# Alternate split units, the second vv from SBUF, and A loads ahead of C loads

## The chip, the cores and the metric

The kernel runs on one core of one Trainium2 chip. The metric is the device time of one execution in microseconds: before the change the median of three runs is 690.73 us (689.88 to 691.08). The page and the trace come from one further, profiled execution.

Engines are named as in the profile: PE is TensorE's matmul and PEld its weight load, DVE is VectorE, ACT is ScalarE, POOL is GpSimd, SP is SyncE, which here only issues DMAs. "PEq", "SPq" and so on are their sequencers.

## The reference

`x` is 8 batches of 3008 rows of 256. Each batch goes through a two-dimensional Fourier transform, of which the real part is kept, and then through a gated feed-forward block with 1536 hidden columns:

```python
def _attn_ref(x):
    X = np.fft.fft(x, axis=1)
    X = np.fft.fft(X, axis=2)
    return X.real

def _moe_ref(x, w_gate, w_val, w_out):
    g = x @ w_gate
    silu = g * (1.0 / (1.0 + np.exp(-g)))
    val = x @ w_val
    return silu * val @ w_out
```

Output: 24064 rows of 256, float32.

## The kernel before

**The mathematics that the kernel uses.** Rows k and M - k of the transform share their cosine and sine products. The kernel therefore computes half of the rows of each batch (H = 1504) as a pair of columns, one in Pt (the part that has the same sign in both rows) and one in Qt (the part whose sign turns), and the feed-forward block makes both output rows from the pair. The transform along the 256 columns is folded into the weights: Wp and Wq are the gate and value weights times cosines and sines, and Wm is Wq times -2 (0 in row 0).

**Folds and transforms.** The rows of x are added and subtracted before they are multiplied. A batch has two sets of rows, A and C, loaded into XA and XC. `fold_steps` gives seven steps for one half of a set: SDf (sum and difference, L165), EOf (L168, L169, L172), Af (L175), CE (L178, L179) and BB (L182 to L184). All run on POOL. `transform` (L559 on) multiplies CE and BB with the tables on PE, ACT copies one half (od, L599), and DVE puts sums and differences into Pt and Qt (L604). `spread` fixes in which unit each fold step is issued, `slot` in which unit each transform.

**Units.** The 12032 pairs are cut into 24 tiles: six of 480 or 512 columns for the first two batches, then 512 each, and 320 in the last (tile 23), which also carries 8 columns for row 0 of each batch. A tile has 12 units, one for each 128 of the hidden columns. The main loop walks over all units. For each it issues some loads on SP (`run_loads`), the unit's first part (`part_a`), four matmuls of the output product of the tile before (`OWork.run`), the second part of the unit before (`part_b`), four more output matmuls, and the fold steps and transforms due. Every engine works through its instructions in this order.

**An unsplit unit** has six matmuls of a tile's width: g and v of the plus row (Wp on Pt, Wq on Qt), then, in `part_b`, Wm on Qt added on top of both, which makes g and v of the minus row. ACT takes Silu of g each time (L764, L782) and DVE multiplies with v straight from PSUM into hp and hm (L765, L783).

**A split unit** has five. e = Wp on Pt and o = Wm on Qt go to two PSUM banks of their own. DVE makes es = e + w0 * bc in SBUF (L752), then vv = es - o/2 for the plus row, called vp in the code (L754), and vv = es + o/2 for the minus row, called vm (L756). Since v is now in SBUF, POOL can make the products hp and hm (L757, L779), with Silu from ACT (L749, L778). bc is row 0 of Qt spread over all partitions: one matmul with `sel` (L880) and an ACT copy (L883) for each tile.

`split(u)` says which units are split: in tiles 3 to 22, units 0, 2, 3, 5, 7 and 9 of a tile, and in tiles 21 and 22 nine of the twelve (`SPLIT_END`). There are 126 in all.

**Buffers.** vv has four buffers (two for each split unit), sgv four, es two, bc two; the PSUM pools of g and v have three banks each, that of the output product two. The evicted output ev has four buffers (L703, L706), which SP stores to DRAM (L709).

**Loads.** `loads` is a list. `load_next` appends the loads of a set as soon as its buffer has been read: 20 for A of one batch (L129, L131), 78 for C of two batches (L140, L143, L145). In each unit `run_loads` issues the first three of the list if A stands at its head, else six. The first fold step of a set issues what is left of its loads and all that stands ahead of them in the list. SP also issues the stores, in the order of the program.

Of the kernel before, what the change touches and what calls it, by code (L numbers as in the profile page):

```python
# [16 lines left out]
Alu = mybir.AluOpType  # L17
# [14 lines left out]
def kernel(  # L32
# [8 lines left out]
    nc = tc.nc  # L41
    B, M, D = x.shape
# [14 lines left out]
    nT = len(wide)  # L57
# [9 lines left out]
    def width(t):  # L67
        return wide[t]

    def tile_of(c):  # L70
        return max(t for t in range(nT) if t0[t] <= c)
# [46 lines left out]
    def up_block(b, j, n):  # L118
        return rows_at(b, 2 * j - 1, [[2 * D, n], [R * D, 4], [1, 2 * D]])

    def down_set(b, a, j, L, n):

        return rows_at(b, R * (a + 1) - 2 * j, [[2 * L * D, n], [-2 * D, L], [1, 2 * D]])
# [3 lines left out]
    def load_a(b, q):  # L127
        X3 = XA.rearrange("p a q d -> p a (q d)")
        return ([lambda h=h: q.dma_start(out=X3[LA * h:LA * (h + 1), 0:4, :],  # L129
                                         in_=up_block(b, JA - LA * h, LA)) for h in range(NA)] +  # L130
                [lambda a=a: q.dma_start(out=X3[:, 4 + a, :], in_=down_set(b, a, JA, LA, NA)) for a in range(4)])  # L131

    def load_c(b, q):
        bb = b % 2
        steps = []
        for qq in range(2):
            p0 = 64 * qq
            for h in range(NC_):
                up = rows_at(b, 2 * (JC - LC * h) - 1 + qq, [[2 * D, LC], [R * D, 4], [1, D]])
                steps.append(lambda p=p0 + LC * h, up=up: q.dma_start(out=XC[p:p + LC, 0:4, bb, :], in_=up))  # L140
            for a in range(4):
                down = rows_at(b, R * (a + 1) - 2 * JC + 1 - qq, [[2 * LC * D, NC_], [-2 * D, LC], [1, D]])
                steps.append(lambda p=p0, a=a, down=down: q.dma_start(out=XC[p:p + NCR, 4 + a, bb, :], in_=down))  # L143
        pm = 64 + NCR
        steps.append(lambda: q.dma_start(out=XC[pm:pm + 1, 0:4, bb], in_=rows_at(b, 0, [[R * D, 1], [R * D, 4], [1, D]])))  # L145
        return steps
# [381 lines left out]
    def pq_tiles(t):  # L528
        if t not in ptile:
            w = width(t) + B if t == nT - 1 else T  # L530
            ptile[t] = (pqp if t < nT - 1 else const).tile([P, w], BF16, name="Pt")
            qtile[t] = (pqp if t < nT - 1 else const).tile([P, w], BF16, name="Qt")
        return ptile[t], qtile[t]
# [181 lines left out]
    state = {}  # L715
    owork = None

    SPLIT = (0, 2, 3, 5, 7, 9)
    SPLIT_END = (0, 1, 2, 4, 5, 7, 8, 10, 11)
    t_end = tile_of((B - 1) * H) + 1  # L720

    bc = {}

    def split(u):

        return 3 <= u[0] < nT - 1 and u[1] in (SPLIT if u[0] < t_end else SPLIT_END)

    def part_a(u):
        t, f = u
        w = width(t) + (B if t == nT - 1 else 0)  # L730
        fs = slice(f * P, (f + 1) * P)
        if f == 0:
            hts[t] = (hp.tile([P, nF, T + B], BF16, name="hp"), hp.tile([P, nF, T], BF16, name="hm"))
        Pt, Qt = pq_tiles(t)

        def mm(ps, Wt, gv, src, start, stop):
            nc.tensor.matmul(ps[:, :w], Wt[:, gv, fs], src[:, :w], start=start, stop=stop,  # L737
                             skip_group_check=True)

        g = psG.tile([P, T], F32, name="g")  # L740
        mm(g, Wp, 0, Pt, True, False)
        mm(g, Wq, 0, Qt, False, True)
        if split(u):
            e = psV.tile([P, T], F32, name="v")
            mm(e, Wp, 1, Pt, True, True)
            o = psV.tile([P, T], F32, name="v")
            mm(o, Wm, 1, Qt, True, True)
            sg = sgv.tile([P, T], F32, name="sgv")
            nc.scalar.activation(sg[:, :w], g[:, :w], AF.Silu)  # L749
            stt = nc.vector.scalar_tensor_tensor  # L750
            es = esp.tile([P, T], F32, name="es")
            stt(es[:, :w], bc[t][:, :w], w0[:, f:f + 1], e[:, :w], op0=Alu.mult, op1=Alu.add)  # L752
            vp = vvp.tile([P, T], F32, name="vv")
            stt(vp[:, :w], o[:, :w], -0.5, es[:, :w], op0=Alu.mult, op1=Alu.add)  # L754
            vm = vvp.tile([P, T], F32, name="vv")
            stt(vm[:, w - 1::-1], o[:, :w], 0.5, es[:, :w], op0=Alu.mult, op1=Alu.add)  # L756
            nc.gpsimd.tensor_tensor(hts[t][0][:, f, :w], sg[:, :w], vp[:, :w], op=Alu.mult)  # L757
            state[u] = (g, vm)
            return
        v = psV.tile([P, T], F32, name="v")  # L760
        mm(v, Wp, 1, Pt, True, False)
        mm(v, Wq, 1, Qt, False, True)
        sg = sgp.tile([P, T], F32, name="sg")
        nc.scalar.activation(sg[:, :w], g[:, :w], AF.Silu)  # L764
        nc.vector.tensor_tensor(hts[t][0][:, f, :w], sg[:, :w], v[:, :w], op=Alu.mult)  # L765
        state[u] = (g, v)

    def part_b(u):
        t, f = u
        w = width(t)  # L770
        Pt, Qt = pq_tiles(t)
        g, v = state.pop(u)
        for gv, ps in ((0, g), (1, v))[:1 if split(u) else 2]:
            nc.tensor.matmul(ps[:, :w], Wm[:, gv, f * P:(f + 1) * P], Qt[:, :w], start=False, stop=True,  # L774
                             skip_group_check=True)
        if split(u):
            sg = sgv.tile([P, T], F32, name="sgv")
            nc.scalar.activation(sg[:, w - 1::-1], g[:, :w], AF.Silu)  # L778
            nc.gpsimd.tensor_tensor(hts[t][1][:, f, :w], sg[:, :w], v[:, :w], op=Alu.mult)  # L779
            return  # L780
        sg = sgp.tile([P, T], F32, name="sg")
        nc.scalar.activation(sg[:, :w], g[:, :w], AF.Silu)  # L782
        nc.vector.tensor_tensor(hts[t][1][:, f, w - 1::-1], sg[:, :w], v[:, :w], op=Alu.mult)  # L783
# [13 lines left out]
    for b in range(2, B, 2):  # L797
        u = slot[(b, 0)] - 1
# [9 lines left out]
    def run_loads(n):  # L808
        for _, fn in loads[:n]:
            fn()  # L810
        del loads[:n]

    def fold_step(what, i, unit):
        kind, b = what
        q, j = divmod(i, 7)
        if i == 0:
            run_loads(max((k + 1 for k, (w_, _) in enumerate(loads) if w_ == what), default=0))
        if j == 0:
            if kind == "A":
                queue[what] = fold_steps(nc.gpsimd, XA, *coef_a(b), q, slice(0, P))  # L820
            else:
                bb = 1 if b == 1 else q
                queue[what] = fold_steps(nc.gpsimd, XC, *coef_c(b), bb, slice(0, P), q_down=bb)
        queue[what].pop(0)()
        if q == LASTQ[kind, b == 1] and j == 1:
            act_at.setdefault(max(unit + 2, 11), []).append(what)

    def load_next(what):
        kind, b = what
        if kind == "A":  # L830
            if b + 1 < B:
                loads.extend((("A", b + 1), fn) for fn in load_a(b + 1, nc.sync))
        else:
            b = b // 2 * 2 + 2
            if b < B:
                loads.extend((("C", b), fn) for fn in load_c(b, nc.sync) + load_c(b + 1, nc.sync))
# [5 lines left out]
    for jb in jobs[1:]:  # L842
        u = slot[jb]
# [27 lines left out]
    loads = []  # L871
# [3 lines left out]
    for i, u in enumerate(units):  # L875
        t, f = u
        if f == 0 and split((t, SPLIT[0])):
            ps = psG.tile([P, T], F32, name="g")
            w = width(t)
            nc.tensor.matmul(ps[:, :w], sel, pq_tiles(t)[1][:, :w], start=True, stop=True)  # L880
            bc.pop(t - 2, None)
            bc[t] = bcp.tile([P, T], F32, name="bc")
            nc.scalar.copy(bc[t][:, :w], ps[:, :w])  # L883
        for fn in before.pop(i, ()):
            fn()
        if i == 10:
            loads[0:0] = ((("A", 1), fn) for fn in load_a(1, nc.sync))
        run_loads(3 if loads and loads[0][0][0] == "A" else 6)
        part_a(u)
        if owork:  # L890
            owork.run(4)
        if prev is not None:
            part_b(prev)
            if prev[1] == nF - 1:
                owork = OWork(prev[0], hts[prev[0]])
                owork.run(4)
        if owork and not (prev is not None and prev[1] == nF - 1):
            owork.run(4)
        for what, j in fold_at.get(i, ()):
            fold_step(what, j, i)  # L900
        for what in act_at.pop(i, ()):
            load_next(what)
        if i in job_at:
            transform(*job_at[i])
        prev = u
# [35 lines left out]
```

## Time and profile before

| what | value |
|---|---|
| median of three runs | 690.73 us |
| profiled execution, its own time | 688.43 us |
| its span on the core | 686.7 us |
| mean granted TensorE clock | 0.995 |
| instructions in the span | 13388 |
| HBM read / written | 29.39 MB / 24.65 MB |
| mean DMA rate over the span | 77 GB/s |

The time is what the runs are compared by; the span is from the first to the last instruction of the profiled execution, and every duration and window of the trace lies within it.

In a group's row stand the line, the engine, the operation, output and inputs, their shapes and the count; behind the bar the busy time in us and the mean ns of one, and behind the next bar the idle time just before them and what ended it. A line number is one of the kernel as printed above. In a timeline's row stand the start and the duration in us, and in brackets how long the engine idled before it and what released it. A row of the waits has who waited for whom, then the total in us, how many times, and the longest.

### The profile page before, as it was taken

Reading aid. Unit: us, or ns where it says so; the run is one execution under the profiler, and the core shown is the slowest. Engines: PE = TensorE matmul, PEld = TensorE weight load, DVE = VectorE, ACT = ScalarE, POOL = GpSimd, SP = SyncE. Lnnn points to the kernel's source line nnn. Section 1 sums busy time; section 2 is a strip of 40 time slices with the busy share of each in tenths; the row PEclk is TensorE's granted clock in tenths of the full one; section 3 lists DMA queues with packets and bytes.
Section 4 is the critical chain, followed back from the end, with each engine's and each line's share of the span. In section 5 each row is a group of like instructions: output and inputs, shape, how many; then the busy total and the mean of one; then the engine's idle time right before and its main releaser. Section 6 shows DMA issues by size and latency. Waiting matters only on the chain.

```text
span 686.7 us, 13388 instructions
## 1 busy us (share of the span) xinstructions
PE 662.1 (96%) x4374; PEld 414.7 (60%) x4374; DVE 513.5 (75%) x919; ACT 432.4 (63%) x764; POOL 570.3 (83%) x558
## 2 busy tenths in 40 slices
PE   7989999999799999999999999999999999999997
PEld 5446665665455666565665666656666666656676
DVE  8886668786567877777777787777777787788862
ACT  7676655665456666565666666666666666666663
POOL 9991977999499999999998998998999655668920
PEclk9999999999989999999999999999999999999999
DMA  9555225323512412235125111117111011111112
GB/s 229 105 87 109 74 59 156 110 67 107 165 31 66 121 47 68 72 95 160 36 62 145 38 44 35 48 40 155 36 48 48 32 41 38 46 32 47 47 47 70
DMA packets 49767, 52.56 MB, mean 77 GB/s; under 512 B 7130, under 2 KB 41026, under 8 KB 49698
## 3 DMA queue, kind: packets, MB, share of 16 engines
q1 hardware_dynamic: 46514, 49.35, 26.4%
q0 software_dynamic: 3184, 2.36, 2.4%
q8 instruction: 34, 0.56, 0.4%
q14 instruction: 35, 0.29, 0.1%
HBM read 29.39 MB, written 24.65 MB: 79 GB/s over the span
## 4 chain that ended last, share of the span: by engine, by line
PE 80%; DVE 8%; POOL 4%; issue 4%; ACT 1%; DMA 1%; SPq 0%; DVEq 0%; ACTq 0%; POOLq 0%
PE o L697 31%; PE v L737 16%; PE g L737 15%; PE g L774 8%; PE v L774 4%; PE v L572 3%; DVE vv L756 2%; DVE Pt L604 1%; PE g L572 1%; POOL hm L779 1%; DVE es L752 1%; DMA out_dram<-ev 1%; DVE vv L754 1%; POOL SDf L165 1%; PE g L880 1%
## 5 line engine op out<-in xcount | busy, mean ns | idle before, releaser
L757 POOL TENSOR_TENSOR hp<-sgv,vv 128x512 bf16<-128x512 f32 (+1 forms) x126 | 160.3, 1274 | 39.9 <-DVE vv L754 26.8
L697 PE MATMUL o<-Wo,hm 128*128 128x256 bf16 (+2 forms) x1140 | 170.5, 274 | 0.0
L697 PE MATMUL o<-Wo,hp 128*128 128x256 bf16 (+2 forms) x1140 | 169.6, 273 | 0.0
L779 POOL TENSOR_TENSOR hm<-sgv,vv 128x512 bf16<-128x512 f32 (+1 forms) x126 | 159.8, 1273 | 9.9 <-ACT sgv L778 8.2
L697 PEld LDWEIGHTS <-hp 128*128 128x128 bf16 (+2 forms) x1140 | 112.0, 98 | 68.2 <-issue 7.8
L697 PEld LDWEIGHTS <-hm 128*128 128x128 bf16 (+2 forms) x1140 | 112.4, 99 | 65.8 <-issue 6.4
L752 DVE SCALAR_TENSOR_TENSOR es<-bc,w,v 128x512 f32<-128x512 f32 (+1 forms) x126 | 93.7, 744 | 52.4 <-PE v L737 52.3
L765 DVE TENSOR_TENSOR hp<-sg,v 128x512 bf16<-128x512 f32 (+2 forms) x162 | 107.8, 665 | 33.0 <-ACT sg L764 32.1
L783 DVE TENSOR_TENSOR hm<-sg,v 128x512 bf16<-128x512 f32 (+2 forms) x162 | 107.4, 663 | 24.2 <-ACT sg L782 15.3
L782 ACT ACTIVATE sg<-g 128x512 f32<-128x512 f32 (+2 forms) x162 | 94.7, 585 | 46.8 <-PE g L774 46.0
L764 ACT ACTIVATE sg<-g 128x512 f32<-128x512 f32 (+2 forms) x162 | 94.5, 583 | 38.2 <-PE g L737 35.6
L737 PE MATMUL v<-Pt,Wp 128*128 128x512 bf16 (+2 forms) x288 | 108.4, 376 | 6.3 <-DVE vv L756 6.2
L737 PE MATMUL g<-Pt,Wp 128*128 128x512 bf16 (+2 forms) x288 | 108.5, 377 | 1.5 <-ACT sgv L778 1.1
L778 ACT ACTIVATE sgv<-g 128x512 f32<-128x512 f32 (+1 forms) x126 | 75.4, 598 | 53.7 <-PE g L774 39.8
L737 PE MATMUL g<-Qt,Wq 128*128 128x512 bf16 (+2 forms) x288 | 108.2, 376 | 0.5 <-DVE Qt L604 0.5
L774 PE MATMUL g<-Qt,Wm 128*128 128x512 bf16 (+2 forms) x288 | 108.1, 375 | 0.0
L754 DVE SCALAR_TENSOR_TENSOR vv<-v,es 128x512 f32<-128x512 f32 (+1 forms) x126 | 87.0, 690 | 18.6 <-POOL hp L757 1.0
L756 DVE SCALAR_TENSOR_TENSOR vv<-v,es 128x512 f32<-128x512 f32 (+1 forms) x126 | 85.7, 680 | 12.9 <-POOL hm L779 12.8
L749 ACT ACTIVATE sgv<-g 128x512 f32<-128x512 f32 (+1 forms) x126 | 75.1, 596 | 30.6 <-PE g L737 23.0
L165 POOL TENSOR_TENSOR SDf<-XA 128x1024 f32<-128x1024 f32 x28 | 66.0, 2363 | 24.8 <-DMA XC<-in_x_dram 14.7
L737 PEld LDWEIGHTS <-Wp 128*128 128x128 bf16 x576 | 56.4, 98 | 45.3 <-issue 7.7
L703 ACT COPY ev<-o 128x512 f32<-128x512 f32 x90 | 52.7, 586 | 34.3 <-PE o L697 29.1
(170 smaller groups left out, 731.0 us busy)
## 6 DMA issues: line engine op xcount, KB each, us to landing
out_dram<-ev SPq DMA_DIRECT2D x96, 128.0 KB
XA<-in_x_dram SPq DMA_DIRECT2D x32, 256.0 KB
XA<-in_x_dram SPq DMA_DIRECT2D x112, 64.0 KB
XC<-in_x_dram SPq DMA_DIRECT2D x210, 16.0 KB
XC<-in_x_dram SPq DMA_DIRECT2D x56, 60.0 KB
out_dram<-ev SPq DMA_DIRECT2D x12, 120.0 KB
out_dram<-ev SPq DMA_DIRECT2D x10, 112.0 KB
XA<-in_x_dram SPq DMA_DIRECT2D x1, 1024.0 KB
```

The lines of the kernel that those rows point to most:

```text
L697: nc.tensor.matmul(ps[:n, j, :], hts[minus][:, f, c:c + n], Wo[:, f, :], start=(f == 0), stop=(f == nF - 1))
L737: nc.tensor.matmul(ps[:, :w], Wt[:, gv, fs], src[:, :w], start=start, stop=stop, skip_group_check=True)
L752: stt(es[:, :w], bc[t][:, :w], w0[:, f:f + 1], e[:, :w], op0=Alu.mult, op1=Alu.add)
L754: stt(vp[:, :w], o[:, :w], -0.5, es[:, :w], op0=Alu.mult, op1=Alu.add)
L756: stt(vm[:, w - 1::-1], o[:, :w], 0.5, es[:, :w], op0=Alu.mult, op1=Alu.add)
L757: nc.gpsimd.tensor_tensor(hts[t][0][:, f, :w], sg[:, :w], vp[:, :w], op=Alu.mult)
L764: nc.scalar.activation(sg[:, :w], g[:, :w], AF.Silu)
L765: nc.vector.tensor_tensor(hts[t][0][:, f, :w], sg[:, :w], v[:, :w], op=Alu.mult)
L774: nc.tensor.matmul(ps[:, :w], Wm[:, gv, f * P:(f + 1) * P], Qt[:, :w], start=False, stop=True, skip_group_check=True)
L779: nc.gpsimd.tensor_tensor(hts[t][1][:, f, :w], sg[:, :w], v[:, :w], op=Alu.mult)
L782: nc.scalar.activation(sg[:, :w], g[:, :w], AF.Silu)
L783: nc.vector.tensor_tensor(hts[t][1][:, f, w - 1::-1], sg[:, :w], v[:, :w], op=Alu.mult)
```

## The change

Four edits are made together.

- `SPLIT` becomes the even units. A new list, `SPLIT_MID`, has eight units and is used in tiles 19 and 20 (`t_folds` is 19). `SPLIT_END`, for tiles 21 and 22, keeps nine units but others. The last tile, which had no split unit, gets the first seven of `SPLIT_MID`; its bc therefore covers the 8 extra columns too.
- The second vv is computed as 2 * es - vp from the two SBUF tiles in place of es + o/2. In the last tile it has the 320 columns of the minus row, while es and vp have 328.
- There are now 96 split units in tiles 3 to 18, 16 in tiles 19 and 20, 18 in tiles 21 and 22, and 7 in tile 23: 137.
- `load_next` puts the loads of A in front of the first C load that is still in the list.

```diff
-    SPLIT = (0, 2, 3, 5, 7, 9)
-    SPLIT_END = (0, 1, 2, 4, 5, 7, 8, 10, 11)
+    SPLIT = (0, 2, 4, 6, 8, 10)
+    SPLIT_END = (0, 1, 3, 4, 6, 7, 9, 10, 11)
+    SPLIT_MID = (0, 1, 3, 4, 6, 7, 9, 10)
     t_end = tile_of((B - 1) * H) + 1
+    t_folds = t_end - 2
...
-        return 3 <= u[0] < nT - 1 and u[1] in (SPLIT if u[0] < t_end else SPLIT_END)
+        t, f = u
+        if t == nT - 1:
+            return f in SPLIT_MID[:-1]
+        return t >= 3 and f in (SPLIT if t < t_folds else SPLIT_MID if t < t_end else SPLIT_END)

     def part_a(u):
         t, f = u
-        w = width(t) + (B if t == nT - 1 else 0)
+        n = width(t)
+        w = n + (B if t == nT - 1 else 0)
...
             vm = vvp.tile([P, T], F32, name="vv")
-            stt(vm[:, w - 1::-1], o[:, :w], 0.5, es[:, :w], op0=Alu.mult, op1=Alu.add)
+            stt(vm[:, n - 1::-1], es[:, :n], 2.0, vp[:, :n], op0=Alu.mult, op1=Alu.subtract)
...
             if b + 1 < B:
-                loads.extend((("A", b + 1), fn) for fn in load_a(b + 1, nc.sync))
+                at = next((k for k, (w_, _) in enumerate(loads) if w_[0] == "C"), len(loads))
+                loads[at:at] = [(("A", b + 1), fn) for fn in load_a(b + 1, nc.sync)]
...
         if f == 0 and split((t, SPLIT[0])):
             ps = psG.tile([P, T], F32, name="g")
-            w = width(t)
+            w = width(t) + (B if t == nT - 1 else 0)
```

In the printed code after the change the lines from L719 on stand 6 or 7 lower: es is L758, vp L760, vm L762, hp on POOL L763, hm on POOL L785.

## The prediction

> **What bounds the kernel now.** I read the page's busy times first, then the chain of waits, then busy time by stage, then the timelines around the places where TensorE stops.
>
> ```profile
> PE 662.1 (96%) x4374; PEld 414.7 (60%) x4374; DVE 513.5 (75%) x919; ACT 432.4 (63%) x764; POOL 570.3 (83%) x558
> ...
> PE 80%; DVE 8%; POOL 4%; issue 4%; ACT 1%; DMA 1%; SPq 0%; DVEq 0%; ACTq 0%; POOLq 0%
> ```
>
> TensorE is the bound: 96% busy, and 80% of the chain. The 83% of POOL is an average over stages that differ, so I cut the span where the first split unit begins (104.4), where the last fold has ended (546), and where POOL has run out of work (654). The columns are the stretch, its length, and busy time and instructions of PE, PEld, DVE, ACT and POOL.
>
> ```profile
> 104.40:546.00 441.60, 428.99 (x2812) 266.05 (x2811) 334.46 (x583) 276.33 (x486) 413.95 (x378) 0.99 0.29 79
> 546.00:654.00 108.00, 106.86 (x703) 66.73 (x702) 87.63 (x148) 70.18 (x122) 72.62 (x58) 1.00 0.13 40
> 654.00:687.00 33.00, 28.88 (x244) 23.81 (x242) 12.70 (x26) 15.48 (x35) 3.72 (x3) 1.00 0.21 61
> ...
> POOL SDf L165 <- DMA out_dram<-ev: 10.0, 1, 10.0
> POOL SDf L165 <- DMA XA<-in_x_dram: 7.9, 1, 7.9
> POOL hp L757 <- DVE vv L754: 7.9, 14, 1.0
> ```
>
> In the fold stage POOL is busy 413.95 of 441.6 us: 27.65 us of slack in all. One wait of 10.0 us is a hole; 2.4 us of the 7.9 us wait (it ends at 106.83, below) lie in the stage. POOL is the second bound here, 3% behind the first. In the last tiles there are no folds and it has 35 us to spare; DVE has 20.
>
> The hole costs TensorE this:
>
> ```profile
> 190.27 0.59 PE L737 MATMUL v<-Pt,Wp 128*128 128x512 bf16 x1 [6.23 <-DVE vv L756]
> ...
> 190.00:200.00 10.00, 9.73 (x46) 5.21 (x46) 6.12 (x11) 4.96 (x10) 10.00 (x10) 0.71 0.08 26
> 200.00:210.00 10.00, 9.86 (x67) 5.61 (x64) 7.49 (x14) 5.45 (x10) 9.92 (x11) 1.00 0.10 28
> ```
>
> 6.23 us of waiting, then ten microseconds at a granted clock of 0.71 in which 46 matmuls ran where the next ten hold 67: another 10 x 21/67 = 3.1 us. Together 9.3 us.
>
> **Part 1: more split units.** A split unit leaves out one 512-column matmul. Tiles 19 and 20 go from 6 to 8 split units, tiles 21 and 22 stay at 9, the last tile (320 columns, 328 with the extra ones) goes from none to 7.
>
> ```profile
> 339.88 0.38 PE L737 MATMUL g<-Qt,Wq 128*128 128x512 bf16 x1
> 340.10 0.38 PE L737 MATMUL v<-Pt,Wp 128*128 128x512 bf16 x1
> 340.57 0.38 PE L737 MATMUL v<-Qt,Wm 128*128 128x512 bf16 x1
> ```
>
> The pitch of a 512-column matmul is 0.22 us. So TensorE saves 4 x 0.22 + 7 x 0.22 x 320/512, less one row matmul for the last tile's bc: 1.7 us. The third row shows what the old spacing cost: units 2 and 3 are both split, and the o matmul starts 0.47 after the e matmul, 0.25 late. Alternate units remove this: 0.25 x 16 tiles = 4 us. Both gains count only where TensorE stays the bound.
>
> **Part 2: the second vv from SBUF.** It reads es and vp, both in SBUF, where it read one operand from PSUM. On DVE:
>
> ```profile
> 341.03 0.74 DVE L752 SCALAR_TENSOR_TENSOR es<-bc,w,v 128x512 f32<-128x512 f32 x1
> 341.91 0.69 DVE L754 SCALAR_TENSOR_TENSOR vv<-v,es 128x512 f32<-128x512 f32 x1
> 342.51 0.68 DVE L756 SCALAR_TENSOR_TENSOR vv<-v,es 128x512 f32<-128x512 f32 x1
> 343.13 0.69 DVE L765 TENSOR_TENSOR hp<-sg,v 128x512 bf16<-128x512 f32 x1
> ```
>
> vv needs the es just written and starts 0.88 after it, 0.13 after its end; the second vv follows 0.60 later because it needs nothing new. Now it needs vp, so it must wait for its end too: 0.69 + 0.13 = 0.82, 0.22 more each. The PSUM bank of o comes free one instruction earlier, which is a gain only if DVE's order is what TensorE waits for.
>
> The larger cost is beside POOL. The trace holds the same opcode with two f32 inputs in SBUF (L320), with POOL at work:
>
> ```profile
> 26.02 0.70 DVE L320 SCALAR_TENSOR_TENSOR XA<-XA,mM 128x376 f32<-128x376 f32 x1
> 27.27 1.32 DVE L324 TENSOR_SCALAR SDf<-XA 128x752 int32<-128x752 int32 x1
> ...
> L320 DVE SCALAR_TENSOR_TENSOR XA<-XA,mM x4: 596/656/708, 26.0 to 33.8; 128x376 f32<-128x376 f32 x4
> ...
> 25.69 0.63 POOL L183 TENSOR_TENSOR BBa<-EOf 128x256 bf16<-128x256 f32 x1
> 26.39 0.39 POOL L184 TENSOR_TENSOR BBa<-SA 128x2 bf16<-128x2 f32 x1
> 26.74 1.45 POOL L168 TENSOR_TENSOR EOf<-SA 128x512 f32<-128x512 f32 x1
> 28.14 0.51 POOL L169 COPY EOf<-SA 128x4 f32<-128x4 f32 x1
> ...
> L168 POOL TENSOR_TENSOR EOf<-SDf x21: 1074/1097/1197, 45.1 to 520.2; 128x512 f32<-128x512 f32 x21
> L169 POOL COPY EOf<-SDf x21: 181/198/221, 46.2 to 521.3; 128x4 f32<-128x4 f32 x21
> L184 POOL TENSOR_TENSOR BBa<-SDf 128x2 bf16<-128x2 f32 x14 | 2.8, 203 | 1.1
> ```
>
> Each side lengthens behind the other. POOL's L184 takes 0.39 instead of 0.20, L168 1.45 instead of 1.10, L169 0.51 instead of 0.20: 0.19, 0.35 and 0.31 lost, 0.28 on average, in turn with L320, L320 and L324; and L320 takes 0.70 against 0.60 while L183 ends. For 512 columns instead of 376 I scale 0.28 by 512/376: 0.39 us of POOL per second vv. Bounds: 0.19 (the smallest loss) and 0.68 (all of the instruction). DVE's own wait has its least row here, 0.10; at most it is the whole of a POOL instruction.
>
> [...]
>
> ```profile
> 104.40:546.00 441.60, 65.24 (x96) 0.99 0.29 79
> ```
>
> This counts L756 in the fold stage: 96 of them, and the change keeps 6 a tile there. 96 x 0.39 = 37 us more for a POOL with 27.65 to spare. So POOL becomes the bound. What is queued behind a blocked POOL instruction is the next hp or hm; vv has four buffers, two units' worth, so DVE then stops at the first vv, and TensorE at the third PSUM bank of v.
>
> ```profile
> L757 POOL TENSOR_TENSOR hp<-sgv,vv 128x512 bf16<-128x512 f32 (+1 forms) x126 | 160.3, 1274 | 39.9 <-DVE vv L754 26.8
> ```
>
> In the last tiles DVE is the tight one. 546 to 654 holds 87.63 us of it in 108, plus about 30 es-to-vv gaps of 0.13 = 4. The change adds 4 units x (0.88 + 0.60 + 0.60 - 1.20) = 3.5, then 34 x 0.22 = 7.5, and 34 waits for POOL. POOL is busy about three quarters there and half of a 1.27 us hp is 0.64, so 0.48 each: 16. Sum 118.6, 10.6 over. As POOL often waits for the same vp and starts no earlier than the second vv, I take half of the wait, which leaves 3 us over, and another 3 for tile 23 and for PSUM banks held longer: +6, bounds -2 (part 1's saving alone) and +14.
>
> **Part 3: A loads ahead of C loads.** The order of the built instructions shows SP's queue changed at one place only: the 20 loads of A for batch 2 now stand in the middle of C's for batch 3. The later loads, those of the hole (A for batch 3) among them, keep their order.
>
> ```profile
> 85.47 5.22 SPq L140 DMA_DIRECT2D XC<-in_x_dram  x15
> ...
> 104.80 0.64 SPq L145 DMA_DIRECT2D XC<-in_x_dram  x1
> 105.54 2.12 SPq L129 DMA_DIRECT2D XA<-in_x_dram  x6
> 107.76 1.15 SPq L709 DMA_DIRECT2D out_dram<-ev  x3
> 108.95 4.21 SPq L129 DMA_DIRECT2D XA<-in_x_dram  x9
> 114.65 0.30 SPq L129 DMA_DIRECT2D XA<-in_x_dram  x1
> 115.17 2.53 SPq L131 DMA_DIRECT2D XA<-in_x_dram  x4
> ...
> 106.83 2.36 POOL L165 TENSOR_TENSOR SDf<-XC 128x1024 f32<-128x1024 f32 x1 [7.90 <-DMA XA<-in_x_dram]
> ...
> 112.39 0.59 ACT L703 COPY ev<-o 128x512 f32<-128x512 f32 x1 [0.78 <-DMA XA<-in_x_dram]
> ```
>
> The 20 moved issues take 2.12 + 4.21 + 0.30 + 2.53 = 9.2 us. C's last load then leaves at 114 instead of 104.8, and the fold that starts at 106.83 starts near 116, with hp and hm of tile 3 behind it. The three stores of 107.76 now stand behind all of C and leave at 114.7, 7 us later; the eviction at 112.39, which already waited 0.78 us for a buffer, waits until about 119, and ACT's Silus behind it. So a hole of 7 to 9 us opens in tile 3. The one at 176 to 186 should shrink: SP does the same total work by 120, while POOL arrives some 10 us later, so about 1 us stays. The hole moves; net about 0 for TensorE, bounds -9 and +9.
>
> **Sum**, against the profiled execution's own 688.43 us (span 686.7, 2.3 below the median 690.73). Fold stage: 413.95 + 37.4 for the shared turns + 11.7 idle until 116 + 1 for the old hole + 4 for what a saturated POOL still idles = 468, +26.4. Last tiles +6, less 1 saved in the last tile. Together +31.4: 719.8 for a profiled execution, 722 for the median.
>
> **Rivals.** (a) TensorE stays the bound. For: POOL's waits for vv (7.9 us in the fold stage) leave room, and at 0.19 a turn 18 us fit in the 27.65. Then part 1's 1.7 and 4 are gained, 685; if the hole vanishes too, 9.3 more, 676. Against: L168 and L169 lost twice that. It decides below about 0.25 us a turn. (b) The turns fit, yet the holes add: the new one opens and the old one stays, since A's loads for batch 3 keep their place: +9.3 - 5.7 = +4, 694 to 700. (c) DVE and POOL bind together: at 0.68 a turn the fold stage takes 413.95 + 65 + 12 + 10 = 501, +59, with +14 at the end: 763; half way between this and the forecast, 743, is its middle. For: DVE waits out a fold's 2.36 us at times and falls behind in order. (d) The second vv doesn't run beside POOL at all, because both hang on vp; it would have to be so in tiles with folds too, where POOL is 94% busy, so I fold it into (a).
>
> **Numbers.** The forecast (705 to 738) 0.50; (a) 0.15, of which 0.02 end within 0.2%, about what a measurement of this kernel can tell from no change; (b) 0.15, of which 0.01; (c) 0.20. Faster 0.13, same 0.03, slower 0.84. The range from 692 to 752 leaves out most of (a) and the top of (c), about 0.2.
>
> **What would show it.** Right: L756's successor well above 0.68 us on average; hp and hm above 1.27; POOL near 100% from tile 4 to tile 18, with TensorE below 93% there; DVE and POOL on the chain where TensorE was; POOL's wait for XC ending near 116. Part 3 is wrong if that wait still ends near 107. Wrong as a whole: hp and hm still at 1.27 and TensorE at 97% in the fold stage; then (a) or (b) holds, told apart by the stall in tile 3 and the one near 185.

## The result, and the profile after

The changed kernel takes 725.31 us (median of 4; 690.6 before): a ratio of 1.0513, interval 1.0494 to 1.0532. Its profiled execution, the slowest of the four, took 727.62 us, span 725.9.

First the page of the changed kernel: busy times, the chain by engine, and the three groups of the split units that the new second vv touches.

```profile
PE 669.5 (92%) x4364; PEld 415.1 (57%) x4364; DVE 586.8 (81%) x930; ACT 434.4 (60%) x765; POOL 650.4 (90%) x580
...
PE 56%; POOL 15%; issue 11%; DVE 9%; DMA 3%; ACT 2%; SPq 2%; DVEq 0%; POOLq 0%; ACTq 0%
...
L763 POOL TENSOR_TENSOR hp<-sgv,vv 128x512 bf16<-128x512 f32 (+2 forms) x137 | 198.2, 1449 | 16.8 <-DVE vv L760 13.5
L785 POOL TENSOR_TENSOR hm<-sgv,vv 128x512 bf16<-128x512 f32 (+2 forms) x137 | 186.4, 1365 | 0.7 <-ACT sgv L784 0.6
...
L762 DVE SCALAR_TENSOR_TENSOR vv<-es,vv 128x512 f32<-128x512 f32 (+2 forms) x137 | 154.5, 1128 | 25.6 <-POOL hm L785 11.8
```

TensorE's part of the chain fell from 80% to 56%, and POOL's rose from 4% to 15%. hp and hm grew from 1.27 us to 1.45 and 1.37 although they do what they did, and the second vv from 0.68 to 1.13.

Then busy time by stage, cut where tile 3 and tile 19 begin and where the last tile begins (columns as in the prediction):

```profile
106.10:582.80 476.70, 437.14 (x2824) 268.32 (x2823) 390.12 (x585) 278.92 (x488) 455.31 (x378) 0.97 0.25 70
582.80:691.50 108.70, 104.56 (x684) 64.93 (x683) 97.16 (x149) 69.18 (x122) 95.05 (x65) 1.00 0.13 40
691.50:726.00 34.50, 29.09 (x238) 23.34 (x237) 20.64 (x34) 15.71 (x36) 20.03 (x19) 1.00 0.20 58
```

POOL does the same 378 instructions in the fold stage as before and is busy 455.31 us where it was 413.95. TensorE is at 92% there, from 97%. A tile begins with ACT's copy of bc, whose starts in the timeline give the length of each tile:

| us | tiles up to 2 | tile 3 | tile 4 | tile 5 | tile 6 | tiles 7 to 18 | from tile 19 on |
|---|---|---|---|---|---|---|---|
| before | 104.4 | 27.0 | 25.5 | 37.4 | 28.8 | 325.0 | 138.6 |
| after | 106.1 | 42.4 | 26.8 | 33.4 | 28.1 | 346.0 | 143.0 |

The old hole was in tile 5 and the new one is in tile 3. Twelve tiles without a hole, 7 to 18, take 21 us more, and the last five 4.5 us more. (The 1.7 us up to tile 2 are not the change: in the runs below, whatever their edits, tile 3 begins somewhere between 104.4 and 106.2 us.)

The hole in tile 3 in the timelines of POOL, ACT, PE and SP:

```profile
123.78 2.34 POOL L165 TENSOR_TENSOR SDf<-XC 128x1024 f32<-128x1024 f32 x1 [23.22 <-DMA out_dram<-ev]
...
124.76 0.58 ACT L703 COPY ev<-o 128x512 f32<-128x512 f32 x1 [11.48 <-DMA out_dram<-ev]
...
125.87 0.79 PE L572 MATMUL g<-Tab,BBa 128*128 128x376 bf16 x2 [9.31 <-ACT sgv L784]
...
92.34 5.84 SPq L129 DMA_DIRECT2D XA<-in_x_dram  x10
...
101.29 7.44 SPq L140 DMA_DIRECT2D XC<-in_x_dram  x12
...
121.34 0.64 SPq L145 DMA_DIRECT2D XC<-in_x_dram  x1
122.09 5.64 SPq L709 DMA_DIRECT2D out_dram<-ev  x12
```

And the same place in windows of ten microseconds (the granted clock is the third number from the end):

```profile
106.10:116.10 10.00, 10.00 (x69) 6.57 (x68) 7.54 (x12) 4.96 (x9) 0.00 (x0) 1.00 0.18 57
116.10:126.10 10.00, 0.69 (x5) 0.28 (x3) 0.00 (x0) 1.06 (x2) 2.32 (x2) 0.69 0.34 102
126.10:136.10 10.00, 8.03 (x29) 2.87 (x28) 4.43 (x8) 3.01 (x6) 10.00 (x10) 0.50 0.33 95
```

The C load leaves SP at 121, the stores behind it at 122; ACT's eviction has waited 11.48 us for a buffer, POOL 23.22 for the load. The trace puts POOL's wait down to a store; the C load at 121.34 is what its instruction reads. In the 20 us from 116.1 TensorE runs 34 matmuls, where 134 would fit at the 67 in ten microseconds that the prediction counts at a granted clock of 1.00: 15 us lost by this estimate, some 40% of it in the ten at a granted clock of 0.50.

### The profile page after: what moved, and what is told of

It reads as the page before. It is cut to its first block, busy times and chain, and to the rows that moved or that the text cites. A ratio compares the mean times of both kernels' runs of the same rounds, so it can differ in the third digit from the quotient of the medians.

```text
span 725.9 us, 13551 instructions
## 1 busy us (share of the span) xinstructions
PE 669.5 (92%) x4364; PEld 415.1 (57%) x4364; DVE 586.8 (81%) x930; ACT 434.4 (60%) x765; POOL 650.4 (90%) x580
## 3 DMA queue, kind: packets, MB, share of 16 engines
q1 hardware_dynamic: 46514, 49.35, 25.5%
## 4 chain that ended last, share of the span: by engine, by line
PE 56%; POOL 15%; issue 11%; DVE 9%; DMA 3%; ACT 2%; SPq 2%; DVEq 0%; POOLq 0%; ACTq 0%
PE o L697 20%; PE g L743 11%; PE v L743 11%; PE g L780 5%; POOL SDf L165 4%; POOL hp L763 4%; POOL hm L785 3%; DVE hm L789 3%; PE v L780 3%; PE v L572 2%; DMA XA<-in_x_dram 2%; DVE vv L760 2%; ACT sgv L784 1%; PE g L572 1%; SPq L143 1%
## 5 line engine op out<-in xcount | busy, mean ns | idle before, releaser
L763 POOL TENSOR_TENSOR hp<-sgv,vv 128x512 bf16<-128x512 f32 (+2 forms) x137 | 198.2, 1449 | 16.8 <-DVE vv L760 13.5
L785 POOL TENSOR_TENSOR hm<-sgv,vv 128x512 bf16<-128x512 f32 (+2 forms) x137 | 186.4, 1365 | 0.7 <-ACT sgv L784 0.6
L697 PE MATMUL o<-Wo,hp 128*128 128x256 bf16 (+2 forms) x1140 | 172.5, 275 | 8.4 <-POOL hp L763 8.4
L762 DVE SCALAR_TENSOR_TENSOR vv<-es,vv 128x512 f32<-128x512 f32 (+2 forms) x137 | 154.5, 1128 | 25.6 <-POOL hm L785 11.8
L758 DVE SCALAR_TENSOR_TENSOR es<-bc,w,v 128x512 f32<-128x512 f32 (+2 forms) x137 | 100.0, 730 | 29.0 <-PE v L743 28.6
L770 ACT ACTIVATE sg<-g 128x512 f32<-128x512 f32 (+2 forms) x151 | 88.9, 589 | 49.1 <-PE g L743 46.8
L760 DVE SCALAR_TENSOR_TENSOR vv<-v,es 128x512 f32<-128x512 f32 (+2 forms) x137 | 93.2, 681 | 30.2 <-POOL hp L763 11.8
L788 ACT ACTIVATE sg<-g 128x512 f32<-128x512 f32 (+2 forms) x151 | 89.3, 592 | 47.0 <-PE g L780 44.9
L784 ACT ACTIVATE sgv<-g 128x512 f32<-128x512 f32 (+2 forms) x137 | 80.7, 589 | 60.5 <-PE g L780 52.2
L789 DVE TENSOR_TENSOR hm<-sg,v 128x512 bf16<-128x512 f32 (+2 forms) x151 | 100.7, 667 | 11.8 <-ACT sg L788 11.7
L771 DVE TENSOR_TENSOR hp<-sg,v 128x512 bf16<-128x512 f32 (+2 forms) x151 | 100.7, 667 | 9.6 <-ACT sg L770 8.8
L755 ACT ACTIVATE sgv<-g 128x512 f32<-128x512 f32 (+2 forms) x137 | 80.6, 588 | 46.4 <-PE g L743 29.8
```

Source lines behind the costliest of these rows:

```text
L697: nc.tensor.matmul(ps[:n, j, :], hts[minus][:, f, c:c + n], Wo[:, f, :], start=(f == 0), stop=(f == nF - 1))
L762: stt(vm[:, n - 1::-1], es[:, :n], 2.0, vp[:, :n], op0=Alu.mult, op1=Alu.subtract)
```

## The experiments

Ratios are to the kernel before, run on the same chip, with 95% intervals.

| run | what | median us | ratio | interval |
|---|---|---|---|---|
| e1 | change, second vv from PSUM | 693.39 | 1.0044 | 1.0029 to 1.0059 |
| e2 | before, second vv from SBUF | 714.09 | 1.0341 | 1.0326 to 1.0356 |
| e3 | before, A loads ahead | 692.51 | 1.0037 | 1.0022 to 1.0051 |
| e4 | before, new split units | 692.44 | 1.0025 | 1.0004 to 1.0046 |
| e5 | before, second vv = o + vp | 694.27 | 1.0055 | 1.0029 to 1.0080 |
| e6 | before, second vv = 2 es - es | 713.34 | 1.0313 | 1.0272 to 1.0355 |
| e7 | change, loads in the old order | 716.53 | 1.0377 | 1.0345 to 1.0408 |
| e8 | new split units, paced loads | 684.33 | 0.9906 | 0.9869 to 0.9943 |
| e9 | before, paced loads | 685.05 | 0.9922 | 0.9893 to 0.9950 |
| e10 | even units in all tiles, paced loads | 682.07 | 0.9876 | 0.9852 to 0.9901 |
| e11 | change, paced loads | 713.41 | 1.0332 | 1.0304 to 1.0359 |
| e12 | e8 once more, beside e9 to e11 | 685.07 | 0.9933 | 0.9910 to 0.9956 |

**e1: the change without the SBUF form.**

```diff
-            stt(vm[:, n - 1::-1], es[:, :n], 2.0, vp[:, :n], op0=Alu.mult, op1=Alu.subtract)
+            stt(vm[:, n - 1::-1], o[:, :n], 0.5, es[:, :n], op0=Alu.mult, op1=Alu.add)
```

> The changed kernel with one part undone: the second vv is es + o/2 from PSUM again; the new split units and the order of the loads stay. Theory (the SBUF form takes turns with POOL, and that is nearly all of the slowdown): 684 to 696 us, hp and hm back at 1.27 us, the stall in tile 3 still there. Rival (the split units or the loads cost the time): 715 us or more.

With one operand back in PSUM, 32 of the 35 us are gone (1.0513 to 1.0044). In e1's page hp and hm take 1.26 us again (a mean that includes seven shorter ones of the last tile) and the second vv 0.67. The stall in tile 3 is still there: the tile takes 41.1 us.

**e2: the SBUF form alone**, the same line the other way round in the kernel before.

> The kernel before with the second vv from SBUF alone. Theory: 712 to 728 us, the second vv near 1.1 us and hp and hm above 1.35 us each. Rival (the slowdown needs the new units or the moved loads): under 700 us.

3.4%, about 24 us. The groups of hp, the second vv and hm in its page:

```profile
L757 POOL TENSOR_TENSOR hp<-sgv,vv 128x512 bf16<-128x512 f32 (+1 forms) x126 | 183.9, 1463 | 23.0 <-ACT sg L782 10.2
L756 DVE SCALAR_TENSOR_TENSOR vv<-es,vv 128x512 f32<-128x512 f32 (+1 forms) x126 | 152.9, 1213 | 25.1 <-POOL hm L779 9.5
L779 POOL TENSOR_TENSOR hm<-sgv,vv 128x512 bf16<-128x512 f32 (+1 forms) x126 | 170.3, 1356 | 2.6 <-ACT sgv L778 2.6
```

POOL is busy 625.8 us here and 570.3 before, with the same work: 55.5 / 126 = 0.44 us for each second vv.

**e3: the loads alone.**

```diff
-                loads.extend((("A", b + 1), fn) for fn in load_a(b + 1, nc.sync))
+                at = next((k for k, (w_, _) in enumerate(loads) if w_[0] == "C"), len(loads))
+                loads[at:at] = [(("A", b + 1), fn) for fn in load_a(b + 1, nc.sync)]
```

> The kernel before with A's loads ahead of C's alone. Theory (the hole moves from 176-186 us to tile 3 and grows a little there): 688 to 697 us, a POOL wait of 15 to 25 us that ends between 115 and 125 us. Rival (the hole is removed): about 681 us.

The hole moves. Tile 3 takes 40.8 us (27.0 before) and tile 5 28.4 (37.4), and the fold in POOL's timeline shows why:

```profile
122.24 2.34 POOL L165 TENSOR_TENSOR SDf<-XC 128x1024 f32<-128x1024 f32 x1 [21.53 <-DMA out_dram<-ev]
```

**e4: the split units alone** (the lists and `split` of the change, the second vv from PSUM, the old loads).

> The kernel before with the new split units alone. Theory (11 matmuls fewer and no two split units in a row, TensorE still the bound): 685 us, 4 to 7 us under the kernel before. Rival (POOL or DVE has no room for 137 split units): 690 us or more.

A miss: no gain, rather 1.7 us lost. Tiles 7 to 18 take 323.5 us instead of 325.0, so even units save about 1.5 there. Tile 5, with its hole, grew from 37.4 to 40.0. And tiles 19 to 21 take 83.6 instead of 80.7, because `SPLIT_MID` and `SPLIT_END` set split units side by side. PE's timeline in tile 19:

```profile
559.26 0.38 PE L743 MATMUL v<-Pt,Wp 128*128 128x512 bf16 x1
559.73 0.38 PE L743 MATMUL v<-Qt,Wm 128*128 128x512 bf16 x1
```

Unit 4 follows the split unit 3, and its o matmul starts 0.47 after its e matmul: the stall that units 2 and 3 used to have, now four times in each of tiles 19, 20 and 21. In those three tiles the o matmul comes late 12 times and loses 4.9 us in all; before it was 5 times and 1.3 us.

**e5 and e6: is it the second SBUF operand, or the wait for vp?** Both in the kernel before. e5 computes the same value as o + vp, with the wait for vp and one operand in PSUM. e6 reads es twice, without the wait; it leaves o out of the minus row.

```diff
-            stt(vm[:, w - 1::-1], o[:, :w], 0.5, es[:, :w], op0=Alu.mult, op1=Alu.add)
+            stt(vm[:, w - 1::-1], o[:, :w], 1.0, vp[:, :w], op0=Alu.mult, op1=Alu.add)
...
+            stt(vm[:, w - 1::-1], es[:, :w], 2.0, es[:, :w], op0=Alu.mult, op1=Alu.subtract)
```

> The kernel before with the second vv as o + vp: the same value, it waits for vp as in the change, but one of its two operands stays in PSUM. Theory (two SBUF operands beside POOL are the cost): within 4 us of the kernel before, hp and hm at 1.27 us, the second vv near 0.68 us. Rival (the wait for vp is the cost): 700 us or more.

> The kernel before with the second vv as 2 es - es: o is left out of the minus row, so its value is es alone; it reads SBUF twice and does not wait for vp. Theory (two SBUF operands): 708 to 718 us, as with the SBUF form alone. Rival (the wait for vp): within 4 us of the kernel before.

From e5 the groups of hp and the second vv, then DVE's timeline, then PE's longest entry among the waits:

```profile
L757 POOL TENSOR_TENSOR hp<-sgv,vv 128x512 bf16<-128x512 f32 (+1 forms) x126 | 160.3, 1274 | 42.1 <-DVE vv L754 28.6
...
L756 DVE SCALAR_TENSOR_TENSOR vv<-v,vv 128x512 f32<-128x512 f32 (+1 forms) x126 | 87.0, 690 | 26.8 <-POOL hm L779 13.9
```

```profile
342.03 0.69 DVE L754 SCALAR_TENSOR_TENSOR vv<-v,es 128x512 f32<-128x512 f32 x1
342.82 0.69 DVE L756 SCALAR_TENSOR_TENSOR vv<-v,vv 128x512 f32<-128x512 f32 x1
```

```profile
PE v L737 <- DVE vv L756: 13.4, 25, 6.1
```

From e6, the same two groups:

```profile
L757 POOL TENSOR_TENSOR hp<-sgv,vv 128x512 bf16<-128x512 f32 (+1 forms) x126 | 180.5, 1436 | 21.9 <-DVE vv L754 11.0
...
L756 DVE SCALAR_TENSOR_TENSOR vv<-es 128x512 f32<-128x512 f32 (+1 forms) x126 | 157.1, 1247 | 17.0 <-POOL hm L779 13.8
```

With one operand in PSUM nothing lengthens: hp 1274 ns, the second vv 690. With two in SBUF and no wait for vp, hp takes 1436 and the second vv 1247, and the time is that of e2. So the second SBUF operand is the cause, for this instruction beside POOL. The wait for vp has a price of its own: the second vv starts 0.79 after the first where it started 0.60 after, and TensorE waits for it 25 times; 0.55%, 4 us.

**e7: the change with the loads in the old order** (e3's edit undone).

> The changed kernel with A's loads behind C's again. Theory (a saturated POOL has no slack in which to make up the 23 us it waits in tile 3, so the order of the loads costs more in the changed kernel than the 2 us that it costs alone): 714 to 721 us. Rival (the parts add up, SBUF form +24, split units +2, loads +2, and the rest is the 11 units more): 722 to 726 us.

From e7 to the change, the loads cost 1.0513 - 1.0377 = 1.4%, 9 us. From e4 to e1 they cost 0.2%, within the intervals. The same move costs more where POOL has no idle time left. The lengths of the tiles show where the difference lies. From the kernel before to e3, tile 3 grows by 13.8 us and tiles 4 to 6 give back 9.7. From e7 to the change, tile 3 grows by 14.7 (27.7 to 42.4) and tiles 4 to 6 give back 4.5. There is less to give back: POOL is already behind in e7 and waits 4.88 us at the old hole, where it waited 10.0 before.

**e8: can the hole be removed?** New split units, second vv from PSUM. A goes ahead of C only from batch 3 on, and then seven loads in a unit instead of three; C's loads from batch 4 on go out three in a unit instead of six. "Paced loads" stands for the three edits together; no run has one of them alone.

```diff
+                at = next((k for k, (w_, _) in enumerate(loads) if w_[0] == "C" and w_[1] >= 4), len(loads))
+                loads[at:at] = [(("A", b + 1), fn) for fn in load_a(b + 1, nc.sync)]
...
-        run_loads(3 if loads and loads[0][0][0] == "A" else 6)
+        kind_b = loads[0][0] if loads else ("A", 0)
+        run_loads((7 if kind_b[1] >= 3 else 3) if kind_b[0] == "A" else (3 if kind_b[1] >= 4 else 6))
```

> The new split units with the second vv from PSUM; A's loads go ahead of C's only from batch 3 on, seven in a unit, and C's from batch 4 on go three in a unit, where it was six. Theory (the hole at 176-186 us is SP being late by the C loads of batches 4 and 5): the POOL wait of 11 us there falls below 5 us and the time to 681 to 688 us. Rival (the landing of A's own loads is the wait): 691 us or more.

In e8's profiled execution, POOL's wait for A of batch 3 is 1.48 us, where e4's was 11.4, and tile 5 takes 29.0 us instead of 40.0. The page's busy times and hm's group, and that fold in POOL's timeline:

```profile
PE 655.7 (96%) x4294; PEld 414.7 (61%) x4364; DVE 517.7 (76%) x930; ACT 434.9 (64%) x765; POOL 591.9 (87%) x580
...
L785 POOL TENSOR_TENSOR hm<-sgv,vv 128x512 bf16<-128x512 f32 (+2 forms) x137 | 171.1, 1254 | 5.8 <-ACT sgv L784 5.7
```

```profile
178.20 2.37 POOL L165 TENSOR_TENSOR SDf<-XA 128x1024 f32<-128x1024 f32 x1 [1.48 <-DMA XC<-in_x_dram]
```

The same kernel was run again as e12, and there the profiled execution has the hole:

```profile
185.94 2.34 POOL L165 TENSOR_TENSOR SDf<-XA 128x1024 f32<-128x1024 f32 x1 [9.35 <-DMA XC<-in_x_dram]
```

There tile 5 takes 35.7 us. A's last load leaves SP at 179.2; in e8 it left at 172.8 and before the change at 180.5. e8's profile is the fastest of its four executions (681.38 us) and e12's the slowest of its twelve (689.77). With paced loads the hole is therefore shorter in some executions and not in all; e9 and e10 lie between, with waits of 6.51 and 5.21 us. What makes SP late in one execution and not in another was not traced.

e8's kernel and the changed one have the same 580 POOL instructions. 650.4 - 591.9 = 58.5 us more in the change, over 137 second vvs: 0.43 each.

**e9 to e12: the parts with paced loads.** e9 has e8's edits of the loads in the kernel before, e11 has them in the changed kernel, and e12 is e8 again. e10 is e8 with

```diff
-        if t == nT - 1:
-            return f in SPLIT_MID[:-1]
-        return t >= 3 and f in (SPLIT if t < t_folds else SPLIT_MID if t < t_end else SPLIT_END)
+        return 3 <= t < nT - 1 and f in SPLIT
```

> The kernel before with the pacing of the loads of the run before alone (A ahead of C from batch 3 on, C three in a unit from batch 4 on). Theory (the hole was SP being late): 680 to 685 us, the whole gain of pacing. Rival (the new split units earn part of it): 686 us or more.

> Paced loads, second vv from PSUM, units 0, 2, 4, 6, 8, 10 split in all tiles from 3 to 22 and none in the last: 120 split units. Theory (in the last tiles DVE has no room for more split units, and they cost 3 us there): 679 to 683 us, 1 to 4 us under the kernel with all 137. Rival (each split unit saves TensorE its matmul): 1 to 3 us above the kernel with 137.

> The changed kernel with paced loads, so that no POOL wait stands in tiles 3 to 6. Theory (turns with POOL): 706 to 714 us, some 25 us above the same kernel with the second vv from PSUM. Rival (the holes are what makes POOL run out): under 700 us.

> The kernel with all new split units, the second vv from PSUM and paced loads once more, beside the two above on one chip: 683 to 686 us.

Paced loads alone bring 5 us of the hole's 9. e10, with 17 split units fewer than e12, is 3 us faster, with intervals that don't meet (0.9876 against 0.9933), and from tile 19 on it takes 137.4 us where e12 takes 140.8: the extra units at the end, set side by side as they are, are a loss even without the SBUF form. That even units help by themselves (e10 against e9, 0.9876 against 0.9922) is likely but not settled, as those intervals touch. e11 keeps the whole price of the SBUF form, 713.41 against e12's 685.07, though its folds wait less for loads in the fold stage (7.9 and 2.9 us, where e12's wait 7.8, 9.4 and 3.1):

```profile
L763 POOL TENSOR_TENSOR hp<-sgv,vv 128x512 bf16<-128x512 f32 (+2 forms) x137 | 200.6, 1466 | 16.6 <-DVE vv L760 13.4
L785 POOL TENSOR_TENSOR hm<-sgv,vv 128x512 bf16<-128x512 f32 (+2 forms) x137 | 182.9, 1340 | 0.6 <-ACT sgv L784 0.6
L762 DVE SCALAR_TENSOR_TENSOR vv<-es,vv 128x512 f32<-128x512 f32 (+2 forms) x137 | 160.7, 1173 | 24.6 <-POOL hm L785 10.8
```

e10, 682.07 us, beats both kernels: 1.2% under before and 6% under the change.

## Why the prediction came out near, point by point

**The price of a turn** (0.39 us, bounds 0.19 and 0.68) was right: 0.43 in the change, 0.44 in e2. It rested on three places in the start-up where other instructions met, and its nearness is in part luck: their losses ran from 0.19 to 0.35, and the third, behind L324, is not of the same kind, since L324 reads one tensor from SBUF and not two. The other two alone give 0.27, or 0.37 scaled.

**POOL becomes the bound of the fold stage**: right. From 126 us to the end of the fold stage its waits sum to about 2 us, and e1 and e5 show TensorE back in front once the second operand is in PSUM. The sum was 468 us with POOL busy 451.4 and idle 16.7; it came out 476.7, with 455.3 and 21.4. The turns account for 3.9 of the 8.7 us that were missing (96 times 0.43 instead of 0.39), the fold that started at 123.8 and not near 116 for 6.0, and the other idle time came out 1.3 smaller. The sum said +31.4; the medians differ by 34.7 and the profiled executions by 39.2, since the one before (688.43) was faster than all four runs beside the change and the one after the slowest of its four. So the median's nearness to 722 owes something to chance. Rival (c), that DVE binds too, holds in part: TensorE's most frequent wait in the change is for DVE's hm (15 times, 15.2 us), and DVE is busy 82% of the stage, from 76%.

**The wait for vp**: 0.22 was forecast, 0.19 measured. It was charged to DVE in the last tiles only. e5 shows that it also costs where TensorE is the bound, 4 us, since TensorE waits there for the second vv, which holds o's bank; in the change o is read by the first vv last, so this part should not apply; no run shows it there.

**The order of the loads**: the mechanism was right, the size was not. "C's last load then leaves at 114" was 121: the 20 loads of A and the C loads behind them went out more slowly than their old durations (12 C loads in 7.44 us, 15 took 5.22 before). "A hole of 7 to 9 us" cost TensorE 15, of which the forecast had left out the clock, although it had counted it for the old hole. "About 1 us stays" of the old one: none did. "Net about 0 for TensorE" held in e3 (+2.6 us) and not in the change, where e7 shows 9, the end of its bounds.

**The gains of part 1** failed. Of "Alternate units remove this: 0.25 x 16 tiles = 4 us" the stall was read rightly: each of tiles 7 to 18 has it once before, 0.25 us, and not once in e4. But that is 3.0 us and those tiles got only 1.5 shorter, as TensorE lost time at other places instead. Among them are waits of 1.3 us for hp from POOL and 1.0 for a vv, which these tiles don't have before; the rest was not taken apart. "TensorE saves 1.7 us" overlooked that the new lists put split units next to each other, so that the stall taken out of the early tiles was put into the late ones, four times a tile. The forecast's sum held 1 us of these gains, since it had POOL as the bound; the rest stood in the rivals. In the changed kernel the failure was hidden by the larger loss. The +5 us for the last tiles came out at 4.5, from both causes together: e4 shows 2.2 (140.8 from tile 19 on against 138.6) without the SBUF form, and e2 2.5 (141.1) with that form alone.

**Rivals (a) and (b)** fell with the price. (b)'s holes did not add, the old one vanished. e1 is the case without the price: 693.39 us, where (a) had 685, since part 1 gained nothing.

**By parts**: e2 +24 us, e4 +2, e3 +3, sum 28; measured 35. Some 7 us are the parts acting on each other: the hole costs 9 instead of 3 once POOL is full.

## What to carry to other kernels

Before an operand moves from PSUM to SBUF on VectorE, count how many tensors the instruction then reads from SBUF and how busy GpSimd is: here the second one cost 0.43 us of GpSimd and 0.45 of VectorE each time, 28 us in all with paced loads (e11 against e12). An algebraic twin with one operand left in PSUM (o + vp for 2 es - vp) cost 4 us here, and es + o/2 none. Loads that were moved ahead in SP's queue delayed what they passed, the stores and their buffers too: C's last load left at 121.34 us instead of 104.80, and an eviction in tile 3 waited 11.48 us for a buffer, where the longest wait of one there had been 0.78. Moving only the later loads, with the queue paced, gained 5 us here; which of the two did it was not separated.

## What the runs showed of the hardware

With two operands in SBUF the second vv takes 1.13 us in the change and 1.21 in e2, and hp 1.45 and 1.46. With one of them in PSUM (e5) the vv takes 0.69 and hp 1.27, as before: there one SBUF operand of this instruction cost POOL nothing. (The number of operands is not all: in the prediction's lines L169 took 0.51 us instead of 0.20 behind L324, which reads one.) How long each side waits is read from the 76 second vvs between 215 and 580 us of the change. The POOL instruction that is running when the vv is due takes as long as its like in e8, within 0.02 us. The vv ends 0.55 us after that instruction (median), where it takes 0.69 alone, and the POOL instruction that follows takes 0.45 us longer (median; 0.32 to 0.51), whichever it is. So the two take turns, and some 0.14 us of a vv pass beside the end of a POOL instruction.

With POOL idle in the hole the SBUF form takes 0.66 us for 480 columns, as the first vv does there (L760, 0.66 at 111.64). Beside POOL the vv's own wait depends on when it comes: against the 0.69 that it takes alone, the second row below waits 0.06 us, the third 1.97, most of a fold of 2.35. hm loses 0.45 us behind either, 1.73 and 1.72 instead of 1.27.

```profile
112.33 0.66 DVE L762 SCALAR_TENSOR_TENSOR vv<-es,vv 128x480 f32<-128x480 f32 x1
...
211.38 0.75 DVE L762 SCALAR_TENSOR_TENSOR vv<-es,vv 128x512 f32<-128x512 f32 x1
...
254.64 2.66 DVE L762 SCALAR_TENSOR_TENSOR vv<-es,vv 128x512 f32<-128x512 f32 x1
...
210.31 1.28 POOL L763 TENSOR_TENSOR hp<-sgv,vv 128x512 bf16<-128x512 f32 x1
211.54 1.73 POOL L785 TENSOR_TENSOR hm<-sgv,vv 128x512 bf16<-128x512 f32 x1
...
254.41 2.35 POOL L165 TENSOR_TENSOR SDf<-XC 128x1024 f32<-128x1024 f32 x1
256.71 1.72 POOL L785 TENSOR_TENSOR hm<-sgv,vv 128x512 bf16<-128x512 f32 x1
```

After the stall of 9.31 us, which ended at 125.9, the granted clock stayed at 0.50 until 136.9, with further waits of TensorE in between; after the 6.23 us before the change, which ended at 190.3, it stayed there until 195.7. It had fallen at 119.9 and at 188.9, 3.3 and 4.9 us after TensorE had stopped, so that it was low for 17.07 and 6.83 us, five and two times the 3.41 us of each of the change's three short lows (from 14.04, 334.89 and 437.29 us). From the end of the stall to the rise of the clock it took 11.0 us in the change, with waits of TensorE of 0.99 and 0.78 us in between, and 5.4 us before the change, with none. Whether those waits kept the clock low for longer was not shown.
